# Longformer attention and a gated FFN on one core: shifted V on ScalarE, small copies off GpSimd's queue, start reordered

## The chip, the cores and the metric

The kernel runs on one core of a Trainium2 chip: TensorE (matmuls; PE in the rows, PEld for its weight loads), VectorE (DVE), ScalarE (ACT), GpSimd (POOL) and SyncE (SP), each with its own queue in program order, and 16 transfer engines that move data between HBM and SBUF. The metric is the time of one execution on the device in microseconds (us), as a median over runs. Times in rows are us from the start of the profiled execution, unless marked ns.

## The reference

Attention over 8 batches, 8 heads, 576 positions of 64 numbers, with a band of 32 to each side and 8 global positions that see and are seen by all; then, on the 4608 rows of 512, a gated feed-forward layer with a gated residual.

```python
scores = (1 / sqrt(64)) * q @ k.T                      # per batch and head
mask = (abs(i - j) <= 32) | is_global[i] | is_global[j]
attn = softmax(where(mask, scores, -1e9))
x = (attn @ v).transpose(0, 2, 1, 3).reshape(4608, 512)
out = x + sigmoid(x @ w_res) * ((gelu(x @ w_gate) * (x @ w_val)) @ w_out)
```

## The kernel before, in words

The 8 batches have 9 windows of 64 queries each, 72 in all. They are worked off in 9 chunks (c) of 8 windows, 512 rows each. For a chunk there are scores for every pair of heads (p) and half chunk (quad), `scores` at L406, then `values` for four tiles of two windows (t, L422), the transposes `turn_x` (L458), and the FFN: `ffn_in` (L469) in 12 steps j of two groups of four matmuls (`g_ps`, `v_ps`), and `ffn_out` (L483) for four tiles, each with a gate and three thirds. A window looks at 128 keys that begin 32 ahead of it; even windows use V as it lies in `ve`, odd ones a copy shifted by 64 rows, `vo`. Scores of chunk c+1 and values run between the output tiles of chunk c. The order of the program is written out by hand, and each engine keeps it.

Keys and queries at global positions are gathered by an index (`gather`, L243), turned, and spread into `kgz` and `qgz` (`spread_qk`, L312); `global_scores` (L372) multiplies them with all of Q and K, `global_exp` (L385) takes exponentials, `global_rows` (L394) multiplies with V, and `vgs` holds the result and the global V rows (`spread_vg`, L323), which `values` reads.

Batch 0 is loaded as float32 by SP and ScalarE's queue (`load_raw`, L152), cast in pairs of heads (`cast_pair`, L338), turned by TensorE (`turn_pair`, L346), and Q is copied into a zeroed `qz` (`prep_qz`, L367). V comes into `vraw` and is cast into `ve` by GpSimd (`cast_v`, L254); then VectorE copies `vo` (L558). Batch 1 comes the same way, but its `vo` by two transfers (`shift_v`, L103). The FFN weights come as 20 pieces of 0.5 MB through 10 staging slots that are borrowed from tiles not yet in use (`load_piece`, `cast_piece`, L132 and L135); before, GpSimd casts all of them. Later batches are loaded as bfloat16 by GpSimd (`load_qk`, L88, ten loads; `load_v`, L95, five) and turned by transposing transfers on SP (`turn_qk`, L361). In FFN of chunk c, batch b = c + 1 is prepared: at j = 8 `load_qk(b + 1)` and `prep_qz(b)`, at j = 9 `spread_qk(b)` and `spread_vg(b)`, at j = 11 `global_scores(b)`.

Masks: `hot` marks the global positions, `sel` sums it over rows into PSUM (`isg`), VectorE makes `nong` from it, multiplies with `band` to `maskw`, and from that makes `hide` for the scores of chunk 0, which TensorE adds with a first matmul by `ident`. `far` and `maskg` keep global columns from being counted twice.

## Time and profile before

| | |
|---|---|
| median of the runs | 450.22 us (450.01 to 450.42) |
| profiled execution, time | 447.17 us |
| profiled execution, span | 445.4 us |
| TensorE matmul busy | 399.4 us, 90% of the span |
| VectorE, ScalarE, GpSimd busy | 222.1, 169.7, 188.7 us |
| mean granted TensorE clock | 0.966 of full |
| read from HBM, written | 39.19 MB, 9.44 MB |

The page of the profile gives each engine's busy time, the span in 40 slices, the chain of work that ended last, and the costliest groups. The timeline lists instructions in order of time; in square brackets stands how long the engine had been idle and who released it. The chain of waits goes back from the end and names what each step waited for.

### The profile page before, as it was taken

To read this page: it belongs to the slowest core of one execution; us is meant where nothing else is said; L and a number is where in the kernel's file an instruction comes from. 1 tells how busy PE (TensorE), PEld (TensorE's weight loads), DVE (VectorE), ACT (ScalarE), POOL (GpSimd) and SP (SyncE) were. 2 spreads that over 40 slices of the span, in tenths; PEclk is the share of its full clock that TensorE was granted. 3 is DMA by queue.
4 is the path that set the end of the run, shared out by engine and by line. 5 is a ranking of instruction groups with operands and counts; after the bars stand their busy time and mean duration, and the time that the engine had idled before them with its cause. 6 is when DMAs were issued, how large, how long until landed. Compare 5 with 4: busy or idle time off the path is not lost.

```text
span 445.4 us, 7416 instructions
## 1 busy us (share of the span) xinstructions
PE 399.4 (90%) x2846; PEld 214.6 (48%) x2846; DVE 222.1 (50%) x400; ACT 169.7 (38%) x275; POOL 188.7 (42%) x239
## 2 busy tenths in 40 slices
PE   2831897899979999999899999998999999999994
PEld 1511545554446445644564465445544654464441
DVE  5758577643615445535463545354535544454421
ACT  3510456422433335333534362335334623533320
POOL 6879834627932544254415642563260120022012
PEclk9965999999969999999999999999999999999998
DMA  8999997914991699369927993999298140021001
GB/s 216 263 337 268 308 173 64 74 47 115 144 123 50 104 156 136 72 101 150 125 80 105 180 83 83 117 163 106 67 123 126 33 76 24 1 70 61 1 24 71
DMA packets 156595, 51.47 MB, mean 116 GB/s; under 512 B 138576, under 2 KB 148816, under 8 KB 156560
## 3 DMA queue, kind: packets, MB, share of 16 engines
q0 software_dynamic: 89456, 11.61, 42.4%
q1 hardware_dynamic: 65488, 38.22, 37.8%
q10 hardware_dynamic: 1616, 1.18, 1.0%
q8 instruction: 22, 0.36, 0.3%
q14 instruction: 13, 0.11, 0.1%
HBM read 39.19 MB, written 9.44 MB: 109 GB/s over the span
## 4 chain that ended last, share of the span: by engine, by line
PE 49%; issue 22%; DMA 11%; POOL 10%; DVE 5%; ACT 2%; SPq 1%; POOLq 0%; ACTq 0%
PE f_ps L500 13%; PE g_ps L473 10%; PE v_ps L477 9%; DMA kt<-k_st 5%; PE r_ps L490 4%; POOL ob L506 3%; PE nd L441 3%; DVE vo L558 3%; PE sc L413 3%; POOL k_st L92 2%; DMA qt<-q_st 2%; PE sg L376 2%; DMA ve<-in_v_dram 2%; PE nd L435 2%; PE sn L398 2%
## 5 line engine op out<-in xcount | busy, mean ns | idle before, releaser
L506 POOL TENSOR_TENSOR ob<-prb,xtok 128x512 f32<-128x512 f32 x36 | 41.8, 1161 | 198.9 <-DVE prb L504 179.6
L481 DVE SCALAR_TENSOR_TENSOR ht<-gsb,v_ps 128x512 bf16<-128x512 bf16 x108 | 74.1, 687 | 95.7 <-PE v_ps L477 90.0
L473 PE MATMUL g_ps<-xt,wg_t 128*128 128x512 bf16 x432 | 110.9, 379 | 0.7 <-ACT xt L466 0.7
L477 PE MATMUL v_ps<-xt,wv_t 128*128 128x512 bf16 x432 | 110.9, 379 | 0.0
L480 ACT ACTIVATE gsb<-g_ps 128x512 bf16<-128x512 f32 x108 | 64.4, 597 | 119.6 <-PE g_ps L473 114.7
L500 PE MATMUL f_ps<-wo_t,ht 128*128 128x512 bf16 x432 | 105.9, 381 | 0.0
L477 PEld LDWEIGHTS <-wv_t 128*128 128x128 bf16 x432 | 42.3, 98 | 51.0
L473 PEld LDWEIGHTS <-wg_t 128*128 128x128 bf16 x432 | 42.1, 98 | 50.8 <-issue 0.8
L500 PEld LDWEIGHTS <-ht 128*128 128x128 bf16 x432 | 39.0, 98 | 35.5 <-issue 0.6
L416 ACT ACTIVATE pt<-sc 128x512 bf16<-128x512 f32 x72 | 42.0, 598 | 27.3 <-PE sc L413 27.2
L493 ACT ACTIVATE rsb<-r_ps 128x512 bf16<-128x512 f32 x36 | 21.5, 596 | 70.0 <-PE r_ps L490 61.5
L420 DVE TENSOR_TENSOR pt<-pt,maskw 128x512 bf16<-128x512 bf16 x64 | 27.2, 425 | 28.1 <-ACT pt L416 26.5
L504 DVE SCALAR_TENSOR_TENSOR prb<-rsb,f_ps 128x512 f32<-128x512 bf16 x36 | 24.7, 685 | 32.8 <-PE f_ps L500 32.6
L92 POOL DMA_DIRECT2D q_st<-in_q_dram x30 | 25.7, 877 | 34.2 <-DMA qt<-q_st 24.1
L490 PE MATMUL r_ps<-wr_t,xt 128*128 128x512 bf16 x144 | 37.8, 386 | 0.0
L413 PE MATMUL sc<-qz,kt 128*128 128x128 bf16 x288 | 29.2, 226 | 2.9 <-ACT pt L416 2.0
L413 PEld LDWEIGHTS <-kt 128*128 128x128 bf16 x288 | 22.5, 101 | 16.8 <-issue 6.2
L100 POOL DMA_DIRECT2D ve<-in_v_dram x35 | 29.9, 871 | 0.0
L435 PE MATMUL nd<-vgs,gt 128*128 128x260 bf16 x80 | 15.5, 285 | 14.0 <-DVE vgs L401 14.0
L92 POOL DMA_DIRECT2D k_st<-in_k_dram x30 | 26.7, 900 | 3.0 <-DMA kt<-k_st 2.3
L455 DVE TENSOR_TENSOR xtok<-nd,rden 128x512 bf16<-128x512 f32 x34 | 23.5, 692 | 1.2
L441 PEld LDWEIGHTS <-pt 128*128 128x128 bf16 x576 | 23.3, 99 | 1.3
(133 smaller groups left out, 337.0 us busy)
## 6 DMA issues: line engine op xcount, KB each, us to landing
out_dram<-ob SPq DMA_DIRECT2D x36, 256.0 KB, 2.1
vo<-ve SPq DMA_DIRECT2D x14, 260.0 KB, 6.2
q_st<-in_q_dram POOLq DMA_DIRECT2D x24, 128.0 KB, 5.9
k_st<-in_k_dram POOLq DMA_DIRECT2D x24, 128.0 KB, 6.4
ve<-in_v_dram POOLq DMA_DIRECT2D x21, 128.0 KB, 8.0
wo_t<-in_k_dram SPq DMA_DIRECT2D x8, 256.0 KB, 6.1
extra<-in_moe_w_out_dram SPq DMA_DIRECT2D x3, 512.0 KB
ve<-in_v_dram POOLq DMA_DIRECT2D x14, 96.0 KB, 7.9
```

The lines of the kernel that those rows point to most:

```text
L92: nc.gpsimd.dma_start(dst[0:n, r, :].rearrange("p (h d) -> p h d", d=D), src[b].rearrange("h s d -> s h d")[128 * r:128 * r + n])
L100: nc.gpsimd.dma_start(t[p0:p1, c, :, 0:D], v[b].rearrange("h s d -> s h d")[s0 + p0:s0 + p1])
L413: nc.tensor.matmul(sc[:, n, :, :], kt[b % 2][:, p, 64 * i:64 * i + 128], qz[b % 2][:, p, :, 64 * i:64 * i + 64], start=(c > 0), stop=(c > ...
L416: nc.scalar.activation(mine, sc, ACTF.Exp, bias=0.0, scale=SCALE)
L441: nc.tensor.matmul(nds[h // 4][:, VG * (h % 4):VG * (h % 4) + VG], view(pt, 0, 128, c0, [[1, 128]]), vw, start=False, stop=(h % 4 == 3 and ...
L473: nc.tensor.matmul(g_ps, wg_t[:, kk, 128 * j:128 * j + 128], x[:, kk, :], start=(kk == 0), stop=(kk == NKT - 1))
L477: nc.tensor.matmul(v_ps, wv_t[:, kk, 128 * j:128 * j + 128], x[:, kk, :], start=(kk == 0), stop=(kk == NKT - 1))
L480: nc.scalar.activation(gsb, g_ps, ACTF.Gelu, bias=0.0, scale=1.0)
L481: nc.vector.scalar_tensor_tensor(ht[:, j, :], gsb, 0.5, v_ps, ALU.mult, ALU.mult)
L490: nc.tensor.matmul(r_ps, xt[c % 2][:, kk, 128 * t:128 * t + 128], wr_t[:, kk, :], start=(kk == 0), stop=(kk == NKT - 1))
L500: nc.tensor.matmul(held["f"], ht[:, j, 128 * t:128 * t + 128], wo_t[:, j, :], start=(j == 0), stop=(j == NFF - 1))
L506: nc.gpsimd.tensor_tensor(ob, prb, xtok[c % 2][:, t, :], ALU.add)
```

## The change

It has these parts.

- The shifted V of batch 0 (`vo`) is made by ScalarE in four copies of two key chunks each, where VectorE made it in two of four chunks.
- At the start, the index load goes to ScalarE's queue, the loads of K and Q come in the order of pairs 0, 1, the rest (-1), 2, 3, and the last Q pair is loaded by SP. VectorE clears all of the tiles of batch 0 ahead of the index step, GpSimd clears `pt` and a part of `vraw`, so that V's first chunk is cast in one piece. ScalarE casts Q of pair 0 and the rest of Q and K, and makes `far`. The gathers of Q and V come between the casts of K and Q. The fills of `blk` and `band` come after these.
- The first mask (`hide`) is made from PSUM at once with a matrix `outside`, with `ident_big` (32768 on the diagonal) in the first matmul of the scores. `nong` comes after the global scores of batch 0, and `maskw` in chunk 0's FFN.
- The scores of batch 0's last pair come after its global scores.
- Batch 1: GpSimd casts both K and Q, the turns begin at j = 8, and ScalarE writes `qz` straight from PSUM.
- Weight pieces 14 to 19 are cast by ScalarE and VectorE among the scores of chunk 1, and 18 and 19 are loaded there too, behind `shift_v(1)`; pieces no longer use the slot in `vo` a third time.
- `spread_qk` and `spread_vg` of batches 2 to 7 go from GpSimd to VectorE.

The core of the diff:

```diff
-    turn_of = list(range(10)) + [2, 3, 4, 8, 9, 2, 3, 4, 8, 9]
+    turn_of = list(range(10)) + [2, 3, 4, 8, 9, 2, 3, 8, 9, 2]
...
-    nc.sync.dma_start(gpi, bass.AP(tensor=g32.tensor, offset=g32.offset, ap=[[0, 16], [2, NG], [1, 1]]))
+    nc.scalar.dma_start(gpi, bass.AP(tensor=g32.tensor, offset=g32.offset, ap=[[0, 16], [2, NG], [1, 1]]))
...
-    for p in (0, -1, 1, 2, 3):
+    for p in (0, 1, -1, 2, 3):
         load_raw(0, "k", p, nc.sync)
-        load_raw(0, "q", p, nc.scalar)
+        load_raw(0, "q", p, nc.scalar if p < 3 else nc.sync)
...
-    zero_wide(qz[0], 64, 64, 0, [[2 * S, NP], [1, S]])
+    zero_q(0)
+    zero_k(0)
+    zero_globals(0)
+    zero_v(0, nc.vector)
+    zero_gt(0, nc.vector)
...
+        for hf in range(2):
+            nc.vector.scalar_tensor_tensor(hide[:, 4 * hf:4 * hf + 4, :],
+                                           isg[:, hf, 0:256].rearrange("p (w c) -> p w c", c=64), -1.0,
+                                           view(outside, 0, 128, 0, [[0, 4], [1, 64]]), ALU.mult, ALU.add)
...
         copy(dst[:, p, c0:c0 + SM].rearrange("c (s r) -> c s r", r=RPP), ps.rearrange("c r s -> c s r"))
+        for u in range(2 * b if what == "q" else 0):
+            copy(qz[b][64 * u:64 * u + 64, p, u, 0:SM].rearrange("c (s r) -> c s r", r=RPP),
+                 ps[64 * u:64 * u + 64].rearrange("c r s -> c s r"))
...
+    other_masks()
+    nc.vector.scalar_tensor_tensor(maskg, far, 1024.5, nong, ALU.is_gt, ALU.mult)
+    nc.vector.tensor_tensor(diag, blk[:, 0:8], blk[:, 8:16], ALU.add)
     global_exp(0, sg, ss)
-    for par in range(2):
-        DVE(vo[0][64 * par:64 * par + 64, 0:4, :, :], ve[0][64 - 64 * par:128 - 64 * par, par:4 + par, :, :])
+    for quad in range(2):
+        scores(0, quad, NP - 1)
+    hot_rows(0)
     spread_v(0, 1)
     spread_vg(0, nc.vector)
+    for c in (0, 2):
+        for par in range(2):
+            ACT(vo[0][64 * par:64 * par + 64, c:c + 2, :, :], ve[0][64 - 64 * par:128 - 64 * par, c + par:c + 2 + par, :, :])
...
-                    spread_qk(b, compact, (b // 2) * 128, {"k": POOL, "q": POOL})
-                    spread_vg(b, nc.gpsimd)
+                    spread_qk(b, compact, (b // 2) * 128, {"k": DVE, "q": DVE})
+                    spread_vg(b, nc.vector)
...
                 if n == 3:
                     work_f[0]()
+                    cast_piece(14, ACT)
+                    load_piece(18)
+                    cast_piece(15, DVE)
+                    load_piece(19)
+                elif n == 5:
+                    cast_piece(16, ACT)
+                    cast_piece(17, DVE)
...
+            cast_piece(18, ACT)
+            cast_piece(19, DVE)
```

On GpSimd in the start, between the pair casts and the first weight cast (`wg_t`, `wv_t`), there stood before:

```order
L289 COPY gt_84<-hot 64x576
L533 TENSOR_SCALAR xtok_90<-iota_f,gpc 128x576
L534 TENSOR_TENSOR xtok_90<-xtok_90 128x576
L245 DMA vgf<-in_v_dram,idx 128x64
L216 MEMSET ve_80 128x40
L217 MEMSET ve_80 32x520
L218 MEMSET ve_80 32x520
L256 CAST ve_80<-vraw 32x8x64
L256 CAST ve_80<-vraw 64x8x64
L256 CAST ve_80<-vraw 128x8x64 x3
L256 CAST ve_80<-vraw 96x8x64
L136 CAST wg_t<-qz_77 128x4x256
```

and now there stands, from the gather of V (`vgf`) on:

```order
L254 DMA vgf<-in_v_dram,idx 128x64
L356 CAST k_st<-wo_t 128x512
L356 CAST q_st<-ht 128x512
L190 MEMSET blk 128x16
L192 AFFINE_SELECT blk<-blk 128x16 x2
L190 MEMSET band 128x64
L192 AFFINE_SELECT band<-band 128x64 x2
L262 CAST ve_80<-vraw 128x8x64 x4
L262 CAST ve_80<-vraw 96x8x64
L136 CAST wg_t<-qz_77 128x4x256
```

The gather of V stands two casts earlier in the list, and the `gt` copy, the two passes over `far` (in `xtok_90`) and the memsets of `ve` are gone from it.

On ScalarE the end of batch 0's start, from the global exponentials (`ptg`, `gt`) to the first Gelu (`gsb`), was only

```order
L388 ACTIVATE ptg_86<-ss 128x5x64
L390 ACTIVATE gt_84<-sg 64x576
L466 COPY xt_88<-tx 128x4x128 x4
L480 ACT_TABLE_LOAD
L480 ACTIVATE gsb<-g_ps 128x512 x4
```

and is now

```order
L406 ACTIVATE ptg_86<-ss 128x5x64
L408 ACTIVATE gt_84<-sg 64x576
L434 ACTIVATE pt<-sc 128x4x2x64 x2
L302 COPY gt_84<-hot 64x576
L588 COPY vo_82<-ve_80 64x1040 x4
L484 COPY xt_88<-tx 128x4x128 x4
L498 ACT_TABLE_LOAD
L498 ACTIVATE gsb<-g_ps 128x512 x4
```

The two exponentials of the last pair, the `gt` copy and the four shifted copies stand ahead of the copies that feed the first FFN matmul.

In chunk 1 VectorE's list around `prep_qz` (the `qz` copy) had

```order
L369 COPY qz_76<-qt_74 64x4x576 x2
L481 SCALAR_TENSOR_TENSOR ht<-gsb,v_ps 128x512
L631 COPY kgc<-tg 128x384
L631 COPY qgc<-tg 128x384
L321 CAST vgb<-vgf 128x3x64
L481 SCALAR_TENSOR_TENSOR ht<-gsb,v_ps 128x512 x2
```

and has now

```order
L387 COPY qz_76<-qt_74 64x4x576 x2
L499 SCALAR_TENSOR_TENSOR ht<-gsb,v_ps 128x512
L655 COPY kgc<-tg 128x384
L655 COPY qgc<-tg 128x384
L334 CAST vgb<-vgf 128x3x64
L330 COPY kgz_154<-kgc 64x4x8 x2
L330 COPY qgz_156<-qgc 64x4x8 x2
L338 TENSOR_TENSOR vgs<-vgb,diag 64x520
L499 SCALAR_TENSOR_TENSOR ht<-gsb,v_ps 128x512 x2
```

Before, the four small copies and the product stood on GpSimd behind the ten loads of `load_qk(3)`.

## Rows read from the trace of the kernel before

**Rows 1.** The page, 40 equal slices: TensorE busy and its granted clock, in tenths

```profile
PE   2831897899979999999899999998999999999994
...
PEclk9965999999969999999999999999999999999998
```

**Rows 2.** Waits of TensorE: engine, line waited for: us in total, times, longest

```profile
PE nd L435 <- DVE vgs L401: 14.0, 1, 14.0
PE sg L376 <- POOL kgz L317: 8.3, 5, 3.6
```

**Rows 3.** Chain of waits, 24 to 51 us: start, length, engine and line

```profile
27.71 11.90 DVE vo L558
...
39.65 1.42 DVE vo L558
...
46.06 0.43 PE nd L435 x2
...
50.09 1.02 PE g_ps L473 x4
```

**Rows 4.** Timeline of GpSimd, V casts and weight cast 11: start, length, engine, line

```profile
24.61 3.62 POOL L256 CAST ve<-vraw 32x512 bf16<-32x512 f32 x6 [3.21 <-DMA vgf<-in_v_dram,idx]
...
39.31 1.21 POOL L136 CAST wv_t<-xtok 128x1024 bf16<-128x1024 f32 x1 [0.25 <-DMA xtok<-in_moe_w_val_dram]
```

**Rows 5.** Timeline near chunk 1's global scores; two windows: stretch, length, busy, clock

```profile
118.05 1.57 DVE L369 COPY qz<-qt 64x2304 bf16<-64x2304 bf16 x2
...
123.20 0.87 POOL L92 DMA_DIRECT2D k_st<-in_k_dram  x1 [0.90 <-DMA kt<-k_st]
...
125.60 2.10 PE L376 MATMUL sg<-qt,kgz 128*128 128x288 bf16 x8 [3.61 <-POOL kgz L317]
...
125.60:128.00 2.40, 2.40 (x26) 1.70 (x27) 0.00 (x0) 0.00 (x0) 1.45 (x3) 0.50 1.97 164
...
130.00:132.00 2.00, 2.00 (x9) 0.98 (x8) 0.59 (x2) 1.09 (x2) 0.00 (x0) 0.56 0.02 1
```

**Rows 6.** Transfers, 14 to 30 us in 40 slices of 0.4 us: GB/s

```profile
GB/s 217 218 218 216 214 205 173 124 221 287 346 351 343 356 353 351 343 356 348 346 353 346 343 366 333 307 343 348 371 338 341 346 351 351 346 348 348 340 346 346
```

**Rows 7.** Timeline of the start: index step, global scores, global exponential of batch 0

```profile
4.36 0.16 DVE L240 SCALAR_TENSOR_TENSOR idx<-hrow,gpi 128x1 int32<-128x1 int32 x1 [1.46 <-DMA gpi<-in_global_idx_dram]
...
21.64 1.14 PE L376 MATMUL sg<-qt,kgz 128*128 128x288 bf16 x8
...
23.64 0.63 ACT L390 ACTIVATE gt<-sg 64x576 bf16<-64x576 f32 x1
```

**Rows 8.** Timeline: three ScalarE copies and casts by size

```profile
6.05 1.90 ACT L251 COPY pt<-none 128x2048 f32<-128x2048 f32 x1
...
62.13 0.67 ACT L614 COPY gt<-hot 64x576 bf16<-64x576 bf16 x1
...
65.97 0.62 ACT L343 CAST q_st<-vraw 128x512 bf16<-128x512 f32 x1
```

**Rows 9.** Timeline of chunk 0: FFN step 9, first and last exponentials

```profile
65.63 1.03 PE L473 MATMUL g_ps<-xt,wg_t 128*128 128x512 bf16 x4
...
77.11 0.60 ACT L416 ACTIVATE pt<-sc 128x512 bf16<-128x512 f32 x1 [0.28 <-PE sc L413]
...
81.24 2.18 ACT L416 ACTIVATE pt<-sc 128x512 bf16<-128x512 f32 x4
```

**Rows 10.** Timeline: load and cast of weight piece 17, and `shift_v(1)`

```profile
50.60 0.37 SPq L133 DMA_DIRECT2D vo<-in_moe_w_out_dram  x1
...
57.83 1.04 POOL L136 CAST wo_t<-vo 128x1024 bf16<-128x1024 f32 x1 [0.73 <-DMA vo<-in_moe_w_out_dram]
...
64.08 0.53 SPq L104 DMA_DIRECT2D vo<-ve  x1
```

**Rows 11.** Timeline: two small VectorE copies beside a GpSimd cast

```profile
59.69 1.14 DVE L317 COPY kgz<-kgc 64x32 bf16<-64x32 bf16 x2
```

**Rows 12.** The page, costliest groups: busy, mean ns, idle before and its releaser

```profile
L481 DVE SCALAR_TENSOR_TENSOR ht<-gsb,v_ps 128x512 bf16<-128x512 bf16 x108 | 74.1, 687 | 95.7 <-PE v_ps L477 90.0
```

More of the change, by code (lines that the diff above doesn't have):

```diff
@@ L230 @@
     nc.vector.tensor_single_scalar(hrow, ip, 3, ALU.logical_shift_right)
-    none = const.tile([128, 1], F32, name="none", tag="none")
-    zero(none)
     sel = const.tile([128, 128], BF16, name="sel", tag="sel")
@@ L249 @@
     gather("k", 0)
-    gather("q", 0)
-    nc.scalar.copy(view(pt.bitcast(F32), 0, 128, 32, [[64, H * CH], [1, 32]]),
-                   view(none, 0, 128, 0, [[0, H * CH], [0, 32]]))
     def cast_v(c, copy):
-        for p0, p1 in ((32, 64), (64, 128)) if c == 0 else (v_rows(c),):
-            copy(ve[0][p0:p1, c, :, 0:D], vraw[p0:p1, c, :].rearrange("p (h d) -> p h d", d=D))
+        p1 = 96 if c == 4 else 128
+        copy(ve[0][0:p1, c, :, 0:D], vraw[0:p1, c, :].rearrange("p (h d) -> p h d", d=D))
     gpc = const.tile([128, 1], F32, name="gpc", tag="gpc")
@@ L262 @@
     nc.vector.tensor_scalar(hot, iota_f, gpc, None, ALU.is_equal)
+    ngp = const.tile([128, 1], F32, name="ngp", tag="ngp")
+    nc.vector.tensor_single_scalar(ngp, gpc, -1.0, ALU.mult)
     diag = const.tile([128, H], BF16, name="diag", tag="diag")
@@ L358, in turn_pair @@
         copy(dst[:, p, c0:c0 + SM].rearrange("c (s r) -> c s r", r=RPP), ps.rearrange("c r s -> c s r"))
+        for u in range(2 * b if what == "q" else 0):
+            copy(qz[b][64 * u:64 * u + 64, p, u, 0:SM].rearrange("c (s r) -> c s r", r=RPP),
+                 ps[64 * u:64 * u + 64].rearrange("c r s -> c s r"))
     def turn_qk(b):
@@ L408, in scores @@
         if c == 0:
-            nc.tensor.matmul(sc, ident, view(hide, 0, 128, 256 * quad, [[64, 4], [0, 2], [1, 64]]),
+            nc.tensor.matmul(sc, ident_big, view(hide, 0, 128, 256 * quad, [[64, 4], [0, 2], [1, 64]]),
                              start=True, stop=False)
@@ L514 @@
     POOL, DVE, ACT = nc.gpsimd.tensor_copy, nc.vector.tensor_copy, nc.scalar.copy
-    zero_wide(qz[0], 0, 64, S, [[2 * S, NP], [1, S]])
-    zero_k(0)
+    cast_pair(0, 0, "q", ACT)
     cast_pair(0, 0, "k", DVE)
-    cast_pair(0, 0, "q", POOL)
-    cast_pair(0, -1, "k", POOL)
-    cast_pair(0, -1, "q", POOL)
-    masks()
-    for p in range(1, NP):
-        for what in "kq":
-            cast_pair(0, p, what, POOL)
-    zero_globals(0)
-    for p in (0, -1):
-        for what in "kq":
-            turn_pair(0, p, what)
-    prep_qz(0, 0, 1)
-    nc.vector.tensor_tensor(diag, blk[:, 0:8], blk[:, 8:16], ALU.add)
-    zero_gt(0, nc.gpsimd)
-    hot_rows(0)
-    nc.gpsimd.tensor_scalar(far, iota_f, gpc, None, ALU.subtract)
-    nc.gpsimd.tensor_tensor(far, far, far, ALU.mult)
-    gather("v", 0)
-    zero_v(0, nc.gpsimd)
-    for p in range(1, NP + 1):
+    for what in "kq":
+        cast_pair(0, 1, what, POOL)
+    gather("q", 0)
+    first_masks()
+    nc.scalar.activation(far, iota_f, ACTF.Square, bias=ngp, scale=1.0)
+    for what in "kq":
+        turn_pair(0, 0, what)
+    prep_qz(0, 0, 1, 0, SM)
+    for what in "qk":
+        cast_pair(0, -1, what, ACT)
+    for what in "kq":
+        cast_pair(0, 2, what, POOL)
+    gather("v", 0)
+    for what in "kq":
+        cast_pair(0, 3, what, POOL)
+    fill(blk, 1.0, [([[-8, 16]], 1, 0, ALU.is_ge, 0.0), ([[8, 16]], -1, 7, ALU.is_ge, 0.0)])
+    fill(band, 1.0, [([[-1, 64]], 1, 0, ALU.is_ge, 0.0), ([[1, 64]], -1, 64, ALU.is_ge, 0.0)])
+    for what in "kq":
+        turn_pair(0, 1, what)
+    scores(0, 0, 0)
+    prep_qz(0, 1, 2, 0, SM)
+    for what in "kq":
+        turn_pair(0, -1, what)
+    prep_qz(0, 0, NP, SM, S)
+    scores(0, 1, 0)
+    for p in range(2, NP + 1):
         if p < NP:
@@ L548 @@
                 DVE(compact[what][:, 0:1, :], got[what])
-        for quad in range(2):
-            scores(0, quad, p - 1)
-        if p == NP - 1:
-            nc.vector.scalar_tensor_tensor(maskg, far, 1024.5, nong, ALU.is_gt, ALU.mult)
+        if p < NP:
+            for quad in range(2):
+                scores(0, quad, p - 1)
     for c in range(5):
@@ L580 @@
     for p in (-1, 0, 1, 2, 3):
-        cast_pair(1, p, "k", POOL)
-    for n in range(12, 20):
+        for what in "kq":
+            cast_pair(1, p, what, POOL)
+    for n in (12, 13):
         cast_piece(n, POOL)
-        if n + 5 < 20:
-            load_piece(n + 5)
+    load_piece(17)
     for c in range(NCH):
```

72 lines of the change are left out of this document (36 added, 36 removed).

## The prediction

> **What bounds the kernel now.** The profiled execution spans 445.4 us and took 447.17 us; the runs have a median of 450.22 us. Differences are worked out in the span and taken off the median. I read the 40 slices first [rows 1]: TensorE is 80% or more busy nearly everywhere from 45 us on, but 30% and 10% in the two slices from 22 to 45 us, where its granted clock falls to half. Then TensorE's list of waits [rows 2]: one of 14.0 us for VectorE's `vgs` (the product with `diag`), and five, 8.3 us together, for GpSimd's `kgz` copy. The others are smaller and nearly all lie in the start. So two places are open, and I read each closely.
>
> The first is the chain of waits from 24 to 51 us [rows 3]: after GpSimd's V casts come VectorE's two copies that make the shifted V (`vo`), 11.90 and 1.42 us, then three short VectorE steps, TensorE again, and at 50.09 the first matmul of the feed-forward part (FFN). The timeline [rows 4] shows why the copy is long: GpSimd's weight casts run back to back behind the V casts, and the copy, begun at 27.71, ends at 39.61, in the 0.25 in which GpSimd waits for a transfer ahead of its cast of 39.31. The same rows show that the V casts began late: GpSimd sat 3.21 until 24.61 for the gather of V.
>
> The second is the end of FFN in chunk 1 [rows 5]: TensorE is out of work at 121.99, 3.61 before it starts the global scores at 125.60, since they need `kgz`, whose copies stand on GpSimd behind five K loads. Then the clock is at 0.50 (1.2 of the two levels 1.2 and 2.4 GHz) for 125.6 to 128 and 0.56 for 130 to 132. The other four waits of this kind, in chunks 2 to 5, are 8.3 - 3.6 = 4.7 together, and the clock stays up there (slices at 9 [rows 1]).
>
> **Part 1: the start, up to the first FFN matmul (50.09).** The V casts no longer wait for the gather, and are 5 instructions instead of 6. When may they run? V moves in small packets at about 215 GB/s; the rate dips at 17 us and then goes to 346 with the weights [rows 6], so V has landed by about 17. GpSimd's list ahead of the casts gets shorter (three casts, a copy and two passes over `far` go, some fills come). So the casts end near 18 instead of 28.23, and no longer decide.
>
> What decides then is the score chain of batch 0, in the profile with its first global score matmul at 21.64 and the end of the global exponentials at 24.27 [rows 7]. It gets later: VectorE clears `qz`, `kgz`, `ve` and `gt` ahead of the index step, which goes from 4.36 to some 5.9 by the lengths of these memsets; the gathered K and Q are cast after `qz` of pair 2, not ahead of it; and the two `nong` steps stand ahead of the global scores. Against this the first mask has two steps less. I take +1.9: global scores at 23.5, exponentials done at 26.2. The `qz` copies of batch 0 stay on VectorE and now fall between other casts; four of them, each held for up to the 0.6 of a K cast, give 0 to 2.4, and I take 1.0: 27.2. Then ScalarE does two more score exponentials (0.60 each [rows 9]; 28.4), `hot_rows` (0.67 [rows 8]; 29.0 in all) and four copies of 64x1040. Between 64x576 at 0.67 and 128x2048 at 1.90 [rows 8] an element of a partition costs 0.84 ns, so one takes 1.06: two are done at 31.1, four at 33.2. The first two tiles of `values` need the first two copies only and run under the others. From the fourth copy to FFN remain tiles 2 and 3 with norm, transposes and copies: 46.06 to 50.09 [rows 3], 4.0. FFN starts at 37.2. **Gain 12.9**, between 10 and 16. The weights are no bound: at 346 GB/s a piece of 0.5 MB takes 1.5, so piece 1 is there at 20 and piece 11 near 36, while FFN uses two pieces in two steps of (65.63 - 50.09) / 9 = 1.73 [rows 3, 9].
>
> The Trainium skill (SBUF — State Buffer, Who interferes with whom) states that VectorE's second port pair, which it shares with GpSimd, is an exclusive lock, given by issue order for one whole instruction. By that the copy would have waited for one cast of some 1.03 and not through eleven, and the part would be worth some 3 and not 13; the 11.90 of the trace disagrees, and the measurement decides.
>
> **Part 2: chunk 0 from FFN on.** FFN step j=8 now carries the first turn of batch 1, and ScalarE writes `qz` of batch 1 straight from PSUM, two copies more for each pair at some 0.58 (an exponential of that width is 0.60 [rows 9]), while its Q casts of 0.62 [rows 8] go to GpSimd. A pair takes ScalarE 1.75 instead of 1.2. Five turns (the small one 1.1), three Gelus of 0.60 and the table load of 1.28 now follow one another: I get the first exponential 12.6 after the end of j=8, against 11.5 in the profile (65.63 to 77.11 [rows 9]): +1.1. Then the last six weight pieces: ScalarE and VectorE cast them between the scores. On ScalarE each is 0.62 plus 512 x 0.84 ns = 1.05; two stand among the exponentials, where it has no gap (the four from 81.24 follow one another in 2.18 [rows 9]): +2.1. Pieces 18 and 19 are loaded only after 14 and 15 are cast, and the third part of the first output tile needs them some 5.5 after that issue. A load took 7.2 from issue to cast when others were queued ahead [rows 10]; here the queue is nearly empty, so I take 0.5 of stall, 0 to 6 as bounds. On SP these loads also stand behind the two transfers of `shift_v`, issued at 64.08 in the profile [rows 10]; the loads are due near 71, so that is no wait. **Loss 3.7**, between 1 and 9.
>
> **Part 3: `spread_qk` and `spread_vg` on VectorE, chunks 1 to 6.** Four small copies and a product, some 1.5 a chunk, leave GpSimd's queue behind its ten loads and stand behind VectorE's `qz` copies. VectorE has about 1.0 free in each FFN step (1.73 less the 0.69 of `ht` [rows 12]), so two steps hide them; without that cover they delay `ht` by 1.5 a chunk. Late next are the transposing transfers of K, on which the K loads of chunk 1 wait: the fourth goes out at 123.20 after 0.90 [rows 5], the fifth about 1.2 later. The stall of 3.61 goes, and with it the half clock from 125.6 to some 131.8, worth half of 6.2; of the 6.7 I leave 1.2 for the last K transfer: 5.5. Chunks 2 to 5 give their 4.7, and I take off 0.3 for `ht`: **gain 9.9**, between 2 and 11.
>
> **Edits at nothing.** The reordered K and Q loads move the same bytes through transfer engines that are full; on SP one Q load takes the place of the index load, and V's loads stand behind it. On ScalarE the index load stands ahead of Q loads that it delays by its issue, before anything there can start. `far` on ScalarE (by 0.67 [rows 8]) and the clearing of `pt` on GpSimd (about 2 by the 1.90) run while the first loads are on the way; without that cover each costs its length once. GpSimd's five more casts for batch 1 cost it 3.0 and are done some 2 before TensorE turns them.
>
> **Sum.** 12.9 - 3.7 + 9.9 = 19.1: span 426.3, profiled time 428.1, median **431.1**.
>
> **Rivals.**
> 1. Transposes take the place of `kgz`: with shorter chunks Q and K of the next batch land after FFN's end, and part 3 gives 2 instead of 9.9: 439.0. For it: the 0.90 [rows 5]. Against: none of the four later waits shows such a transfer behind it.
> 2. Pieces 18 and 19 come late, in both engines' order ahead of the next tile's work, a stall of 6 instead of 0.5: 436.6. For it the 7.2 [rows 10]; against it the empty queue.
> 3. The start does better: the score chain is no later than now and no copy is held (2.9 less), and part 2 costs 1 instead of 3.7: 425.5.
> 4. The change doesn't do what it says: `qz` of batch 0 still is eight SBUF-to-SBUF copies on VectorE, among casts that now come 8 us earlier. Held for a cast of 0.6 each, they add 5: 436.1. Against: the weight casts are then paced by transfers of 1.5 and leave 0.5 between them.
> 5. Slower: the copies of `kgz` and `qgz` on VectorE are held while GpSimd issues its ten loads (some 0.9 each), as `vo` was by the casts. VectorE then holds `ht`, and TensorE stops for 9 less the 3 that are free in three steps: 6 in each of chunks 1 to 5, +30, and nothing of part 3 is left: 450.2 - 9.2 + 30 = 471. It decides from 1.9 a chunk on, where 5 x 1.9 eats the 9.2 of parts 1 and 2. For it: two `kgz` copies took 1.14 beside a cast [rows 11]. Against: the two long `qz` copies of 118.05 took 1.57 in the middle of such loads [rows 5].
>
> The Trainium skill (SBUF — State Buffer, SBUF: two separate sides) warns that such a VectorE copy locks GpSimd out of writing the descriptors of its loads, which is rival 5 from the other side and speaks against moving copies there; the 1.57 does not show it.
>
> **How the numbers follow.** Forecast 0.52, rivals 1 to 5: 0.13, 0.11, 0.12, 0.07, 0.05. The forecast's own range is 427 to 436. With rivals 1 to 4 it is 424 to 439, which leaves out rival 5 and the ends of the others, under 2 in 10. A measurement of this kernel can tell about 0.2% (0.9 us) from no change. All but rival 5 lie below 449.3; for rivals 1, 2 and 4 at once (439 + 5.5 + 5) I leave 0.01 each to no change and to slower: faster 0.93, same 0.01, slower 0.06.
>
> **What would show it.** Right: V casts done before 20; four ScalarE copies of about 1.06, the last ending near 33; first FFN matmul at 36 to 39; no row of TensorE waiting for `kgz`; the clock up around chunk 1's global scores. Wrong: ScalarE copies far over 1.06 (held as VectorE's was); a stall over 2 ahead of the third part of the first output tile; a wait of the global scores for Q or K of over 1 in several chunks; VectorE copies of `kgz` over 0.5.

## The result, and the profile after

The changed kernel takes **426.57 us** (median of 4 runs, 426.05 to 426.98) against 450.12 of the kernel before beside it: a ratio of 0.948, with a 95% interval of 0.946 to 0.950. The prediction was 431.1, in a range of 424 to 439. The profiled execution took 426.46 and spans 424.7 (445.4 before); its granted clock has a mean of 0.990 (0.966 before).

| stage in us, by the first matmul of the feed-forward part (FFN) in chunks 0 and 1 | before | after | gained | predicted |
|---|---|---|---|---|
| start, to FFN of chunk 0 | 50.09 | 36.87 | 13.2 | 12.9 |
| FFN of chunk 0 to FFN of chunk 1 | 50.6 | 53.9 | -3.3 | -3.7 |
| FFN of chunk 1 to the end | 344.7 | 333.9 | 10.8 | 9.9 |
| span | 445.4 | 424.7 | 20.7 | 19.1 |

FFN of chunk 1 starts at 100.72 before and at 90.79 after, by these rows of the two timelines, the kernel before first:

```profile
100.72 1.03 PE L473 MATMUL g_ps<-xt,wg_t 128*128 128x512 bf16 x4
...
90.79 1.03 PE L491 MATMUL g_ps<-xt,wg_t 128*128 128x512 bf16 x4
```

Next come the page's 40 slices of the changed kernel, TensorE busy and its granted clock in tenths, against [rows 1]:

```profile
PE   2578986999999999999999999999999999999994
...
PEclk9998998999999999999999999999999999999999
```

Slices 3 and 4, at 3 and 1 before, are now at 7 and 8. The clock no longer falls to half there, nor in slice 12; a smaller dip is new in slice 7 (64 to 74 us). The list of TensorE's waits (engine, line waited for: us in total, times, longest) answers [rows 2]:

```profile
PE isg L290 <- DVE vgb L307: 6.7, 1, 6.7
PE sc L431 <- ACT pt L434: 3.7, 3, 1.5
...
PE nd L453 <- DVE vgs L419: 1.0, 1, 1.0
...
PE ss L399 <- DMA kt<-k_st: 0.5, 1, 0.5
```

The 14.0 for `vgs` is down to 1.0, and the five waits for `kgz`, 8.3 together, are gone. What is longest now lies at the very start, where TensorE's first matmul waits for VectorE's first steps (6.7; 5.3 before). The timeline of the start answers [rows 3, 4, 7] (start, length, engine, line, tiles, and in brackets the idle time ahead and its releaser):

```profile
16.94 2.41 POOL L262 CAST ve<-vraw 128x512 bf16<-128x512 f32 x4
...
23.52 1.24 PE L394 MATMUL sg<-qt,kgz 128*128 128x288 bf16 x8 [0.60 <-DVE nong L298]
...
27.91 4.30 ACT L588 COPY vo<-ve 64x1040 bf16<-64x1040 bf16 x4
...
36.87 1.02 PE L491 MATMUL g_ps<-xt,wg_t 128*128 128x512 bf16 x4 [0.67 <-ACT xt L484]
```

The V casts run from 16.94, no longer behind the gather; the global scores come at 23.52; ScalarE's four copies take 1.06 each, one every 1.07, and end at 32.21; FFN starts 4.7 later. For the turn from chunk 0 to batch 1, these rows of the timeline answer [rows 9], two of ScalarE and two of TensorE:

```profile
64.66 0.60 ACT L434 ACTIVATE pt<-sc 128x512 bf16<-128x512 f32 x1
...
68.80 1.06 ACT L136 CAST wo_t<-extra 128x1024 bf16<-128x1024 f32 x1
...
71.11 1.96 PE L416 MATMUL sn<-ve,ptg 128*128 128x260 bf16 x10
...
74.57 0.80 PE L453 MATMUL nd<-vgs,gt 128*128 128x260 bf16 x4
```

Two windows of it (stretch, length, busy time of TensorE, its loads, VectorE, ScalarE and GpSimd, granted clock, DMA share, GB/s):

```profile
62.80:70.00 7.20, 3.75 (x51) 2.52 (x49) 2.76 (x6) 6.65 (x11) 6.59 (x9) 1.00 1.98 158
70.00:75.00 5.00, 4.49 (x25) 2.71 (x25) 3.04 (x7) 3.80 (x6) 1.86 (x2) 0.66 0.82 239
```

In the kernel before, `sn`, the first product of the next tile and a window of the same work were:

```profile
82.62 1.28 PE L398 MATMUL sn<-ve,ptg 128*128 128x260 bf16 x10
...
84.69 0.60 PE L435 MATMUL nd<-vgs,gt 128*128 128x260 bf16 x4
...
82.00:87.00 5.00, 4.89 (x49) 3.30 (x49) 3.19 (x7) 1.42 (x3) 2.53 (x3) 1.00 0.75 61
```

From FFN's start the first exponential comes 27.8 later, where it was 27.0. From there to `sn` it takes 6.45 (5.51 before, with `sn` at 82.62), and from `sn` to the first product of the next tile 3.46 (2.07 before, to 84.69). The granted clock is 0.66 between 70 and 75, which is the lower level of 1.2 GHz for two thirds of the stretch; before, the same work (82 to 87) had 1.00.

### The profile page after: what moved, and what is told of

It is laid out like the page before. It is cut to its first block, busy times and chain, and to the rows that moved or that the text cites. A ratio compares the mean times of both kernels' runs of the same rounds, so it can differ in the third digit from the quotient of the medians.

```text
span 424.7 us, 7431 instructions
## 1 busy us (share of the span) xinstructions
PE 396.5 (93%) x2846; PEld 214.5 (50%) x2846; DVE 217.5 (51%) x433; ACT 180.0 (42%) x291; POOL 169.9 (40%) x202
## 4 chain that ended last, share of the span: by engine, by line
PE 68%; issue 17%; ACT 4%; DMA 4%; DVE 3%; POOL 2%; ACTq 0%; POOLq 0%; SPq 0%
PE f_ps L518 16%; PE g_ps L491 16%; PE v_ps L495 16%; PE r_ps L508 5%; PE nd L459 4%; PE sc L431 3%; POOL ob L524 2%; DMA ht<-in_q_dram 2%; PE sn L416 2%; PE nd L453 2%; DMA kt<-k_st 2%; PE sg L394 1%; ACT qz L375 1%; PE ss L399 1%; PE tx L483 1%
## 5 line engine op out<-in xcount | busy, mean ns | idle before, releaser
L438 DVE TENSOR_TENSOR pt<-pt,maskw 128x512 bf16<-128x512 bf16 x64 | 27.2, 425 | 29.0 <-ACT pt L434 27.8
L473 DVE TENSOR_TENSOR xtok<-nd,rden 128x512 bf16<-128x512 f32 x34 | 23.5, 691 | 1.2
L459 PE MATMUL nd<-ve,pt 128*128 128x65 bf16 x320 | 23.2, 195 | 0.0
```

The costliest lines, as they stand in the source:

```text
L459: nc.tensor.matmul(nds[h // 4][:, VG * (h % 4):VG * (h % 4) + VG], view(pt, 0, 128, c0, [[1, 128]]), vw, start=False, stop=(h % 4 == 3 and ...
```

## Experiments

The kernel before, run beside each of these, had medians of 449.7 to 451.1, with single executions from 446 to 455. A kernel's own median stands against those; where a difference is under 2 us I read it from the stages of the traces, which are one execution each. How far a stage repeats can be seen from stages whose program several kernels share: FFN of chunk 0 starts at 35.93 to 36.87 in six traces; from FFN of chunk 1 to the end it takes 344.7 to 345.5 in the four with the spread on GpSimd, and with it on VectorE 333.1 to 334.6 in nine and 336.6 in the tenth (experiment 8).

**1. The shifted V alone.** Of the whole change, only the four ScalarE copies:

```
-    for par in range(2):
-        DVE(vo[0][64*par:64*par+64, 0:4, :, :], ve[0][64-64*par:128-64*par, par:4+par, :, :])
     spread_v(0, 1)
     spread_vg(0, nc.vector)
+    for c in (0, 2):
+        for par in range(2):
+            ACT(vo[0][64*par:64*par+64, c:c+2, :, :], ve[0][64-64*par:128-64*par, c+par:c+2+par, :, :])
```

> The kernel before, with one thing changed: the shifted V (vo) is made by ScalarE in four copies of 64x1040, behind VectorE's two small steps on vgs, instead of by VectorE in two of 64x2080. The V casts stay late (their end at 28.2). My theory: the starved copy alone made the 14.0 us wait. ScalarE is free at 24.3, its copies run 27.5 to 31.8 at 1.07 each, FFN starts 4.0 behind them at 36 to 37 (50.09 before), the median falls by 12 to 14, to 436 to 438. Rival (the early V casts and the shorter list ahead of them are worth about half of part 1): FFN starts at 41 to 43 and the median falls by 7 to 9. Rival (ScalarE's copies are held by GpSimd's casts as VectorE's was): copies of 3 or more, FFN past 45.

It took 436.66 (ratio 0.973, 0.966 to 0.980), span 434.4. The view of tile `vo` (shortest, median and longest in ns, first and last start):

```profile
L561 ACT COPY vo<-ve x4: 1056/1056/1057, 27.5 to 30.7; 64x1040 bf16<-64x1040 bf16 x4
```

Its timeline:

```profile
38.16 1.02 PE L473 MATMUL g_ps<-xt,wg_t 128*128 128x512 bf16 x3 [0.67 <-ACT xt L466]
```

The V casts still wait for the gather here (GpSimd sits 3.5 until 25.11), and yet FFN starts at 38.16, 11.9 earlier than before, though 1.2 past the 36 to 37 that I expected: TensorE's `sn` waits 4.2 for these casts. With the copies moved, all other edits of the start together are worth the 1.3 from there to 36.87 (up to 0.9 more by the other traces of that start). ScalarE's copies were held by nothing here: all four took 1.06 beside V casts and a train of weight casts (back to back, without a gap) like the one in which VectorE's took 11.90.

**2. The spread alone.** `spread_qk` and `spread_vg` of chunks 1 to 6 on VectorE in the kernel before:

```
-                    spread_qk(b, compact, (b // 2) * 128, {"k": POOL, "q": POOL})
-                    spread_vg(b, nc.gpsimd)
+                    spread_qk(b, compact, (b // 2) * 128, {"k": DVE, "q": DVE})
+                    spread_vg(b, nc.vector)
```

> The kernel before, with spread_qk and spread_vg of the chunks 1 to 6 on VectorE; nothing else. My theory: no wait of TensorE for kgz is left, no half clock in chunk 1's score stage, and the median falls by 9 to 11 to 439 to 441. Rival (transposing transfers take the place of kgz): falls by 2. Rival (VectorE's small copies are held while GpSimd issues its ten loads): rises by 5 or more, kgz copies over 0.9 each.

It took 437.25 (0.973, 0.968 to 0.978), span 435.2, of which 333.9 lie behind FFN of chunk 1: the same as in the changed kernel, and 10.8 less than before. Its row of the timeline:

```profile
101.32 1.03 PE L473 MATMUL g_ps<-xt,wg_t 128*128 128x512 bf16 x4
```

In the view of tile `kgz`:

```profile
L317 DVE COPY kgz<-kgc x14: 154/172/949, 60.4 to 331.8; 64x32 bf16<-64x32 bf16 x14
```

A window over chunk 1's scores:

```profile
125.00:128.00 3.00, 2.95 (x26) 1.73 (x26) 1.26 (x3) 2.83 (x6) 0.82 (x2) 1.00 1.61 238
```

The clock is at 1.00 where it was at 0.50 [rows 5], and a copy of `kgz` has a median of 0.172; the one of 0.949 is batch 1's, beside the casts of chunk 0 as in [rows 11]. Rivals 1 and 5 fall. The two single edits take 11.0 and 10.2 off the span, 21.2 together, where the whole change takes off 20.7; by the medians they take off 13.7 and 13.1, where it takes off 23.6. So no run shows a gain on balance by the rest of the change.

**3. Is the copy starved, slowed, or only late?** The kernel before in two forms: in the first the V casts go ahead of V's gather in GpSimd's order, in the second VectorE's two copies are cut in four of the shape of experiment 1, in their old place. The edit of the first:

```
-    gather("v", 0)
     zero_v(0, nc.gpsimd)
...
     for c in range(5):
         cast_v(c, POOL)
+    gather("v", 0)
```

> The kernel before, with the gather of V moved behind the V casts in GpSimd's order, so that the casts start some 3.2 earlier (21.4 in place of 24.6). The two vo copies stay on VectorE. If a copy starves for as long as GpSimd's casts follow one another: the weight casts start some 2 earlier but still have a backlog of landed pieces, so the first copy still takes 8 to 10 and ends at 36 to 38, in the first gap of GpSimd's; FFN starts at 46 to 48, the time falls by 2 to 4. If VectorE gets its turn after one cast, whatever else was wrong lay in the late casts: the first copy takes under 3 and FFN starts before 41.

> The kernel before, with VectorE's two vo copies of 64x2080 cut into four of 64x1040; nothing else. If a copy waits for a gap of GpSimd's (starvation): the first of the four takes nearly all of the 11.9 and ends at about 39.6, the other three take at most 1.6 each; FFN at 50 to 53. If the copy runs all the time at a small share of the port: the four take about 3 each. If the lock goes by turns, one cast at a time: about 1.6 each from the first on, 6.4 together, and FFN starts at about 43.

They took 443.25 and 447.99 (one run each); FFN starts at 46.09 and 50.19. The copies in the view of tile `vo`, and the GpSimd casts at which the long one ends, early casts first:

```profile
L558 DVE COPY vo<-ve x2: 1424/5712/9999, 25.3 to 35.3; 64x2080 bf16<-64x2080 bf16 x2
```

Its timeline:

```profile
33.69 1.03 POOL L136 CAST wg_t<-extra 128x1024 bf16<-128x1024 f32 x1
34.83 1.35 POOL L136 CAST wv_t<-extra 128x1024 bf16<-128x1024 f32 x1
```

Then the four copies:

```profile
L559 DVE COPY vo<-ve x4: 725/978/11555, 26.8 to 40.0; 64x1040 bf16<-64x1040 bf16 x4
```

Its timeline:

```profile
38.60 1.04 POOL L136 CAST wg_t<-xt 128x1024 bf16<-128x1024 f32 x1
39.76 1.06 POOL L136 CAST wv_t<-xtok 128x1024 bf16<-128x1024 f32 x1
```

With early casts the train of weight casts starts earlier, and the copy sits in it all the same: 10.00, to the first small gap (34.72 to 34.83). Of four copies not each is slow: one takes 11.56, half the data for the time of the whole, and ends after the gap of 39.64 to 39.76; the others take 0.73 to 1.15. So a copy is not slowed evenly, it is kept out. I had expected the first to be the long one; it was the third, while the first two ran beside the V casts and took 0.80 and 0.73. In the kernel before too the copy ended at 39.61, a little after the gap of 39.06 to 39.31, in which the prediction puts its end, and not in it; the cast behind the gap took 1.21 for 1.03.

**4. Back to VectorE, with GpSimd's casts spaced.** The changed kernel with the same four copies on VectorE (`ACT(vo...` to `DVE(vo...`):

> The changed kernel with the four vo copies given back to VectorE; all else stays, so the V casts end at 20.4 and GpSimd's weight casts wait some 0.5 for a transfer ahead of nearly each. My theory (a copy starves only as long as casts follow one another without a gap): each copy lasts until the next gap, 1.0 to 1.6, the four 4 to 6.4 together; they begin at 27.9 and end at 32 to 34.5 (32.2 on ScalarE); FFN starts at 37 to 39.5 instead of 36.9 and the median rises by 0 to 2.5, far less than the 11 to 12 that the same move was worth in the kernel before. Rival (a VectorE copy loses to GpSimd whatever the spacing): one copy of 5 or more, the median rises by 5 to 11.

It took 435.31 (0.970, 0.966 to 0.974), 8.7 more, which is the rival's number, but not by its mechanism. The copies were quick; two thirds of the loss lie 17 us later. The view of tile `vo`:

```profile
L588 DVE COPY vo<-ve x4: 423/789/1153, 28.6 to 31.5; 64x1040 bf16<-64x1040 bf16 x4
```

Its timeline:

```profile
48.20 6.05 DVE L338 TENSOR_TENSOR vgs<-vgb,diag 64x520 bf16<-64x520 bf16 x1
...
52.66 1.03 POOL L136 CAST wr_t<-vo 128x1024 bf16<-128x1024 f32 x1
53.64 1.50 POOL L136 CAST wr_t<-extra 128x1024 bf16<-128x1024 f32 x1
```

From its list of TensorE's waits:

```profile
PE g_ps L491 <- DVE ht L499: 4.1, 1, 4.1
```

The four copies took 3.2 together beside casts that wait for transfers. FFN started at 39.75, 2.9 later: the copies began 0.7 later in this execution, and VectorE's product of `sn`, which the next tile needs, stands behind them. From there to FFN of chunk 1 it took 59.9 in place of 53.9. For VectorE's product `vgs` of batch 1 now began at 48.20, inside GpSimd's train of ten Q and K casts and two weight casts (47.09 to 55.14), and took 6.05 for 0.70. It stands ahead of `ht`, and TensorE stopped for 4.1. In the changed kernel the product runs at 45.32 and the last `kgz` copy ends at 46.47, while the train starts at 46.33 (timeline of the changed kernel):

```profile
45.32 0.70 DVE L338 TENSOR_TENSOR vgs<-vgb,diag 64x520 bf16<-64x520 bf16 x1
...
46.03 0.44 DVE L330 COPY kgz<-kgc 64x32 bf16<-64x32 bf16 x2
...
46.33 0.60 POOL L354 CAST k_st<-wo_t 64x512 bf16<-64x512 f32 x1
```

Behind the stop the granted clock was 0.57 from 56 to 60, so the loss is more than the wait.

**5. The same product put into the train on purpose.** In the changed kernel the product and the `kgz` copies go from FFN step 3 to step 5:

```
-                elif j == 3:
-                    spread_vg(1, nc.vector)
-                    spread_qk(1, compact, 0, {"k": DVE, "q": ACT})
                 elif j == 5:
+                    spread_vg(1, nc.vector)
+                    spread_qk(1, compact, 0, {"k": DVE, "q": ACT})
                     hot_rows(1)
```

> The changed kernel with VectorE's product vgs and two kgz copies for batch 1 emitted two FFN steps later (step 5 for step 3 of chunk 0); nothing else. In the changed kernel they end at 46.47, and GpSimd's train of ten Q and K casts and two weight casts runs from 46.33 to 53.9. My theory (in the run with vo on VectorE the 8.7 came from this product, which began at 48.20 inside the train and took 6.05): the product now begins at 47 to 49, lasts until the train's end near 52 to 54 (3 to 6 us for 0.70), TensorE stops for 2 to 5 of it, and the median rises by 2 to 7. Rival (VectorE gets its turn after one cast, as in the run with vo on GpSimd, where two such steps took 1.02 and 1.45): each of the three steps takes at most 1.3 and the median rises by less than 1. Rival (the 8.7 had another cause): no change, no long product.

It took 432.25 (0.963, 0.955 to 0.970), 5.7 more. VectorE's timeline:

```profile
47.27 6.21 DVE L338 TENSOR_TENSOR vgs<-vgb,diag 64x520 bf16<-64x520 bf16 x1
53.50 1.10 DVE L330 COPY kgz<-kgc 64x32 bf16<-64x32 bf16 x2
```

From its list of TensorE's waits:

```profile
PE v_ps L495 <- DVE ht L499: 4.6, 1, 4.6
```

From FFN of chunk 0 to FFN of chunk 1 it took 61.0 for 53.9, with a granted clock of 0.50 from 56 to 60. So the train explains most of experiment 4's loss, and the changed kernel escapes it by the order of VectorE's steps, with no time to spare. Here and in experiment 4 the product ended inside the train's last cast, which took 1.5 for 1.04, and no gap is to be seen ahead of that cast.

**6. A break in the train.** In the kernel of experiment 5, one of GpSimd's five load issues of V goes into the middle of the train, behind the sixth cast:

```
-    load_v(1)
+    load_v(1, 0, 4)
     for p in (-1, 0, 1, 2, 3):
+        if p == 2:
+            load_v(1, 4, 5)
         for what in "kq":
             cast_pair(1, p, what, POOL)
```

> The kernel of the run with the late product, with one of GpSimd's five load issues of V (0.86 each, no cast) moved from ahead of the train of casts to its middle, behind the sixth of the ten Q and K casts; no other change. The train then starts near 45.5, the issue stands at 48.8 to 49.7, and the product starts near 47.3 as before. Theory (VectorE is let in where the train breaks, whatever stands in the break): the product ends by 50 and takes 1.5 to 2.8 in place of 6.21, the kgz copies follow in the break or behind one cast, TensorE's stop shrinks from 4.6 to under 1.5, and the median falls from 432.3 to 427 to 429. Rival (only the end of the train or a wait of GpSimd lets it in; writing a load's descriptors holds VectorE too): the product still takes 5.5 to 7 and the median stays within 1 of 432.3. Rival (VectorE's turn comes at random): the product takes under 1.3 and ends ahead of the issue.

My theory fell. Timeline of VectorE and GpSimd:

```profile
47.62 8.41 DVE L338 TENSOR_TENSOR vgs<-vgb,diag 64x520 bf16<-64x520 bf16 x1
...
50.46 0.78 POOL L100 DMA_DIRECT2D ve<-in_v_dram  x1
...
54.45 1.03 POOL L136 CAST wr_t<-extra 128x1024 bf16<-128x1024 f32 x1
```

The issue stands at 50.46 to 51.24, and the product waits through it to the end of the last cast (55.48) and ends at 56.03. The four executions took 432.4, 433.3, 436.0, and one 425.3, which is the changed kernel's level; in that one the product presumably was let in, but only the first of them has a trace (TensorE waits 6.1 for `ht` in it). So in this trace a load issue was no break. A load issue alone doesn't hold such a product either: in the changed kernel it took 0.70 at 45.32, while GpSimd issued loads of V (41.97 to 46.28) and cast nothing. That a step can be kept out in one execution and not in the next of the same program fits the four times, and is not shown.

**7. The weight pieces back on GpSimd.** In the changed kernel:

```
-    for n in (12, 13):
+    for n in range(12, 20):
         cast_piece(n, POOL)
-    load_piece(17)
+        if n in (13, 14, 15):
+            load_piece(n + 4)
...
-                    cast_piece(14, ACT)
-                    load_piece(18)
-                    cast_piece(15, DVE)
-                    load_piece(19)
...
-                    cast_piece(16, ACT)
-                    cast_piece(17, DVE)
...
-            cast_piece(18, ACT)
-            cast_piece(19, DVE)
```

> The changed kernel with the last six weight pieces cast by GpSimd ahead of the Q and K loads of batch 2, as in the kernel before, instead of by ScalarE and VectorE among the exponentials of batch 1. My theory: two casts of 1.06 leave ScalarE's exponentials and the matmuls behind them wait less, so sn starts about 0.9 earlier against the first exponential, and TensorE's half clock at 71 to 75 (1.4) goes: the median falls by 1.5 to 2.5, to 424 to 425. Rival (the casts only fill time of ScalarE that nothing waits for): no change. Rival (GpSimd's casts hold VectorE, and the Q and K loads go out 5 to 6 later): rises by 1 to 5, with TensorE waiting for transfers in chunk 1.

It took 424.45 (0.946, 0.943 to 0.949): 2.1 less than the changed kernel by the medians, whose intervals overlap; by the trace FFN of chunk 0 to FFN of chunk 1 takes 51.9 in place of 53.9, and 51.9 again in the first kernel of experiment 10, which has the same edit. `sn` in the timeline:

```profile
69.84 1.60 PE L416 MATMUL sn<-ve,ptg 128*128 128x260 bf16 x10
```

Two of its windows:

```profile
66.00:70.00 4.00, 3.61 (x29) 2.64 (x28) 2.95 (x6) 3.77 (x8) 2.90 (x4) 0.64 0.08 20
70.00:75.00 5.00, 5.00 (x45) 3.13 (x43) 2.44 (x5) 0.68 (x2) 5.00 (x7) 0.95 1.94 123
```

`sn` follows the first exponential (64.17) by 5.67, 0.8 sooner than in the changed kernel, and the next tile 2.38 behind `sn` starts 1.1 sooner. I had expected the half clock to go. It stayed, and now lies under the scores at 66 to 70, where TensorE also waits for ScalarE, and costs less.

**8. `qz` of batch 1 back on VectorE.** In the changed kernel the copies from PSUM in `turn_pair` go out, and `prep_qz` comes in behind the turns of each pair:

```
                         for what in "kq":
                             turn_pair(1, p, what)
+                        if p >= 0:
+                            prep_qz(1, p, p + 1)
```

> The changed kernel with qz of batch 1 copied by VectorE from qt, as in the kernel before, instead of by ScalarE from PSUM; the casts stay on GpSimd. My theory (ScalarE bounds the turns, 0.6 to 0.8 lost there): the first exponential of batch 1 comes 0.5 to 0.9 earlier against the first turn, the median falls by 0.5 to 0.9. Rival (TensorE and VectorE's kt bound the turns): within 0.3. Rival (VectorE's copies are held by GpSimd or hold ht): rises by 0.5 to 2.

It took 426.17 (0.948, 0.944 to 0.952; 423.9 to 427.8): no difference that the times can show. In the trace the first exponential follows the first turn by 10.66 (52.05 to 62.71), where it was 12.16 in the changed kernel (0.5 to 0.9 earlier expected, 1.5 found), and the stage takes 53.1 in place of 53.9. Of 1.5 at the exponentials 0.8 is left at the next FFN.

**9. The shifted V on GpSimd**, all four copies right behind its V casts:

```
     for c in range(5):
         cast_v(c, POOL)
+    for c in (0, 2):
+        for par in range(2):
+            POOL(vo[0][64*par:64*par+64, c:c+2, :, :], ve[0][64-64*par:128-64*par, c+par:c+2+par, :, :])
...
-    for c in (0, 2):
-        for par in range(2):
-            ACT(vo[0][64*par:64*par+64, c:c+2, :, :], ve[0][64-64*par:128-64*par, c+par:c+2+par, :, :])
```

> The changed kernel with the four vo copies on GpSimd right behind its V casts, ahead of the weight casts. My theory (ScalarE's row of global exponentials, two score exponentials, hot_rows and four copies is what sets the start of FFN): copies of 1.0 to 1.4 end by 26, ScalarE is free at 27.9, and FFN starts at 32.5 to 34 instead of 36.9; the weight casts begin 4 to 5.6 later, and pieces 0 and 1 are still cast by 28. The median falls by 2.5 to 4.5. Rival (the later weight casts push the loads of the reused buffers and of batch 1 back, and the gain of the start is given back at the turn to batch 1): FFN starts earlier but the median falls by under 1. Rival (GpSimd's copies slow VectorE's work on the global scores): FFN not before 36.

The six executions took 425.5 to 436.6 (median 431.98). The profiled one, the fastest, has FFN at 36.59, within the changed kernel's 35.93 to 36.87, where I had expected 32.5 to 34. Timeline of VectorE and GpSimd:

```profile
27.21 1.02 DVE L334 CAST vgb<-vgf 128x64 bf16<-128x64 f32 x1
28.27 1.45 DVE L338 TENSOR_TENSOR vgs<-vgb,diag 64x520 bf16<-64x520 bf16 x1
...
28.14 1.04 POOL L136 CAST wg_t<-xt 128x1024 bf16<-128x1024 f32 x1
29.12 1.50 POOL L136 CAST wv_t<-xtok 128x1024 bf16<-128x1024 f32 x1
```

GpSimd's copies ended at 25.83 and ScalarE was free, as expected. But the weight casts then had a backlog and ran without a gap, and VectorE's steps for `vgs` (0.18 and 0.70 elsewhere) were held for one cast each; TensorE waited 2.4 for them. Here VectorE had its turn after one cast; the product of the same size for batch 1 waited to the train's last cast or past it in experiments 4 to 6. The executions of up to 436.6 would fit a step kept out for a train; they have no trace, so this is not shown.

**10. Away from the train, and half of the shifted V on GpSimd.** First the kernel of experiment 7 with VectorE's steps of chunk 0 in another order (product and `kgz` copies in FFN step 0, mask rows in step 1, the clearing of `qz` in step 2); then the same with two of the four `vo` copies on GpSimd, behind its V casts. Of the first:

```
                 if j == 0:
-                    zero_q(1)
+                    zero_globals(1)
+                    spread_vg(1, nc.vector)
+                    spread_qk(1, compact, 0, {"k": DVE, "q": ACT})
...
                 elif j == 2:
-                    zero_k(1)
-                    zero_gt(1, nc.vector)
-                    zero_globals(1)
+                    zero_q(1)
                 elif j == 3:
-                    spread_vg(1, nc.vector)
-                    spread_qk(1, compact, 0, {"k": DVE, "q": ACT})
+                    zero_k(1)
+                    zero_gt(1, nc.vector)
```

> The changed kernel with the last six weight pieces on GpSimd (as in the run before) and VectorE's steps of chunk 0 in another order: the product vgs and the kgz copies of batch 1 in FFN step 0, the mask rows in step 1, the long clearing of qz in step 2. All of VectorE's steps that read and write SBUF alone then end by 43.5, 3 ahead of GpSimd's train in place of 0 to 1. Theory: the median stays at that of the run with the pieces on GpSimd (424.5, within 0.7), and no run stands more than 1.5 above the lowest. Rival (the order fills VectorE in steps 0 to 2 so that ht comes late): 0.5 to 1.5 slower, TensorE waiting for ht at 40 to 46.

> The kernel of the run with the new order of chunk 0, and beside it the first two vo copies on GpSimd right behind the V casts, the other two on ScalarE. Theory (ScalarE's row sets the start of FFN, and only four copies on GpSimd made so long a train that VectorE's steps for vgs were held): GpSimd's two copies end near 23, its weight casts have caught up with the transfers by 27; ScalarE ends at 30.0 in place of 32.2, FFN starts at 34.5 to 35.3, and the median is 1.2 to 2.2 below the kernel without it, 422 to 423.3. Rival (VectorE's products for vgs are held again, 1 to 2.5): FFN at 36 to 37.5, no gain. Rival (one of them waits out a train): FFN past 38.

The first took 424.97 (0.946, 0.941 to 0.952; 423.0 to 426.3). In its profile the steps end at 40.36, far from the train at 47.35 (timeline of VectorE, then GpSimd):

```profile
39.24 0.76 DVE L338 TENSOR_TENSOR vgs<-vgb,diag 64x520 bf16<-64x520 bf16 x1
40.01 0.35 DVE L330 COPY kgz<-kgc 64x32 bf16<-64x32 bf16 x2
...
47.35 0.60 POOL L354 CAST k_st<-wo_t 64x512 bf16<-64x512 f32 x1
```

It costs nothing against experiment 7, but its runs spread by 3.3, more than the 1.5 that I expected from it, so it doesn't show a steadier time. The second took 424.79 (0.945, 0.940 to 0.951): no gain, by a third way of the same cause. The two GpSimd copies held VectorE's `qz` of the last pair, so the global scores came late (timeline of VectorE):

```profile
21.82 2.19 DVE L387 COPY qz<-qt 64x512 bf16<-64x512 bf16 x2 [0.35 <-ACT qt L373]
```

From its list of TensorE's waits:

```profile
PE sg L394 <- DVE nong L298: 2.0, 1, 2.0
```

FFN starts at 37.00. What ScalarE was spared, VectorE paid.

## Why the prediction was right, point by point

**Part 1** holds in its steps: V casts done at 20.35 (near 18 predicted, and before 20 as a sign; the last cast waited 0.40 for V at 19.74, so V had not landed by 17, but the casts are off the path), global scores at 23.52 (23.5), copies at 1.06 (1.06), their end at 32.21 (33.2), FFN at 36.87 (37.2). Two errors partly cancel: the `qz` copies cost no extra 1.0 on the path, and from the last copy to FFN it took 4.7 in place of 4.0. The sum doesn't divide the gain among the edits: experiment 1 shows that the copy kept out alone carries 11.9 of the 13.2, with the V casts as late as before. With the copy still on VectorE, earlier casts were worth 4.0 (experiment 3, FFN at 46.09). The edits taken at nothing (order of the loads, the first mask, the clearing) were not undone one by one; with the rest of the start they make the 1.3. GpSimd's five more casts, also taken at nothing, cost nothing only because VectorE's product was done before the train that they lengthen (in experiments 4 and 5, where it was not, this stage lost 6.0 and 7.1).

**Part 2** is right in size (3.3 for 3.7), in part by luck: one of its three terms held, two were too large, and a cost that it left out made up for them. The turns cost 0.8 (1.1 predicted; the terms listed for the 12.6, that is 1.1, 4 x 1.75, 3 x 0.60 and 1.28, add up to 11.2, while the trace has 12.25 from the end of j=8 at 52.41). The ScalarE casts cost 0.9 up to `sn` (2.1 predicted). The stall for pieces 18 and 19 (0.5) didn't come: the three parts of the first output tile show no wait of TensorE for a load. In its place came 1.4 between `sn` and the next tile, in which `sn` took 1.96 for 1.28, and the first third of the output tile 1.91 for 1.02: the lower clock, which I had only looked for in part 3. Ahead of it TensorE had been busy 3.75 of 7.20 us, and 4.67 of 7.20 at the same place before (75.25 to 82.45), where the clock stayed up. Experiment 7 gives back 2.0 of the 3.3.

**Part 3** holds: 10.8 for 9.9, the clock up, no wait for `kgz`. Of the 1.2 that I kept for the last K transfer one wait of 0.5 is to be seen. Experiment 2 gives the same 333.9 for this stretch with nothing else changed, and the other traces lie far enough apart from those with the spread on GpSimd (333.1 to 336.6 against 344.7 to 345.5).

**The median** came out 4.5 under the forecast. Of that, 1.6 are the three parts. The other 2.9 are the step "differences are worked out in the span and taken off the median": the profiled execution of before was 3.05 faster than its median (447.17 against 450.22), that of after equals its own (426.46 against 426.57). With the span's 426.3 and what lies around it, the sum's own profiled time was 428.1, nearer than 431.1. The result lies 0.4 below the 427 to 436 given for the forecast alone and inside the wide range.

**The rivals.** Experiment 2 excludes 1 and 5: no transposes take the place of `kgz`, and small VectorE copies among load issues are not held (0.172); nor are the issues, for K loads take 0.89 on average in the changed kernel and 0.90 before. Rival 2's stall doesn't appear. Rival 3 names nearly the right time, but of its premises only one came (no copy was held); the global exponentials end at 26.24 (24.27 before), and part 2 cost 3.3, not 1. Rival 4's copies weren't held beyond a cast; its opposing reason, casts paced by transfers, is what experiment 4 shows for `vo`: 3.2 for four copies.

**The lock.** The Trainium skill (SBUF — State Buffer, Who interferes with whom) says that the engine that issues first has the shared port pair for one whole instruction. Where GpSimd's casts are spaced, and in experiment 9, the rows agree: 0.4 to 1.5 for a step, which is held for one cast at most. In a train without gaps they disagree in six cases: 11.90, 10.00, 11.56, 6.05, 6.21 and 8.41. The first three ended 0.2 to 0.5 after the train's first gap (0.1 to 0.25), the next two inside its last cast, the last one 0.55 after it. What decides between one cast and the whole train is open: products of one size had both, and one of the four executions of experiment 6, without a trace, had the total of a product that was let in. The same section's statement that a VectorE step with two SBUF inputs also contends fits the product, and `ht`, with one of its inputs in PSUM, kept its mean of 0.685 beside all these casts.

## What to carry to other kernels

By these runs a VectorE copy, or a product of two SBUF tiles, is at risk wherever GpSimd has a backlog of casts: price it at up to the whole train, not at one cast, and give it to ScalarE or place it where GpSimd waits for transfers. When such a step is moved or an engine ahead of it gets faster, look for the next VectorE step that now meets the train: a product that began 2 to 3 us later cost 6 to 7 here. Read each stage by its first matmul, and compare stages that share a program over several traces: they repeated within 1 to 4 us here, where executions of one kernel spread by up to 11.
